# Choosing, by a table, which engine multiplies half spectra and gate products in a recurrence-then-convolution kernel

## The chip, the cores and the metric

The kernel runs on one core of a Trainium2 chip. Time is the device time of one launch in microseconds; lower is better. The kernel before takes 476.47 us, the median of 3 runs (476.25 to 478.01).

A core has five engines that run their own instruction streams in order and wait for each other by semaphores: PE (TensorE, matrix products, writes PSUM; its weight loads are listed as PEld), DVE (VectorE), ACT (ScalarE), POOL (GpSimd) and SP (SyncE), which here issues the transfers. In this kernel only DVE and ACT read PSUM; POOL works on SBUF alone.

## The reference

For each of 4 batches of 6272 time steps and 256 channels, a gated linear recurrence, then a long convolution with a filter as long as the sequence, between two projections, with a product of three factors:

```
sig = 1.0 / (1.0 + np.exp(-f_logit))
f = lower_bound[None, None, :] + (1.0 - lower_bound[None, None, :]) * sig
i = 1.0 - f
for t in range(S):
    h = f[:, t] * h + i[:, t] * x[:, t]
    y[:, t] = h
...
proj = x @ w_proj                      # x is the y above
x1, x2, x3 = (proj[..., :D].copy(), proj[..., D:2 * D].copy(), proj[..., 2 * D:].copy())
X2 = np.fft.rfft(x2, n=S, axis=1)
H = np.fft.rfft(filter_fft, n=S, axis=0)[None, :, :]
x2_conv = np.fft.irfft(X2 * H, n=S, axis=1)
y = x1 * x2_conv * x3
return (y @ w_out).astype(np.float32)
```

## The kernel before

The sequence length 6272 is 49 x 128. The Fourier transform of each channel is made of two short transforms done as matrix products, over the 128 first and over the 49 then, with a column order that needs no twiddle factors between them. Channels are taken in 16 units u of 8 pairs.

The stages of one batch, with the names that stand in the code:

- `hgrn` (lines 299 to 357), 13 chunks of up to 512 steps: SP loads f_logit and x into FL and XT (`load`); ACT makes the sigmoid (L311); POOL multiplies the two (`u`, L313); PE transposes both into PSUM (`su`, L325); ACT, or sometimes DVE, makes the factor f in fTs (L338, L340); DVE scans along time into HA (`scan`, L346). HA holds the states in f16. The first 3072 of them are copied behind the last one (`wrap`, L354 to L357), so that a strided read may pass the end; this is done by POOL or ACT.
- `phase_p` (L664): PE projects the states with the middle third of w_proj, in 13 groups (`P`, L673); ACT or DVE copies PSUM into X2 (`x2`).
- `phase_f1` (L681): PE makes the first transform of unit u (`F1`, L686); ACT or DVE copies it into A (`A`), a ring of NA = 4 units that lies inside HA. `mini` (L694) makes the zero frequency for four units together.
- `unit` (L729): the product with the filter's spectrum. SP loads the spectrum Hu of the unit from DRAM if it is not held (`H`, L723; NH = 3 buffers). PE makes the second transform (`F2`, L745) into two PSUM banks, one for each half o. DVE multiplies each bank by Hu, reading every spectrum value twice, into PP (`prod`, L758; NP = 2 buffers). POOL fills the one column left out (`slot`, L750). PE makes the first inverse transform (`I2`, L768), which needs both halves and the slot; ACT or DVE copies it into Th (`Th`).
- `gate` (L360), 13 chunks and two halves of the channels: PE makes x1 and x3 (`x13`, L373), each into one PSUM bank; ACT or DVE copies both to x1s and x3s in f32 (`xs`; x1 is scaled by ZS), two buffers in turn; POOL multiplies them into zt in f16 (`z`, L389).
- `phase_o` (L789), 13 groups: PE makes the second inverse transform (`I1`, L802); DVE multiplies PSUM by zt into ys (`y`, L808), for which all 26 z products of the batch must be done; PE multiplies by w_out (`proj`, L820); ACT or DVE scales into osb (`o`, L272), three buffers; SP stores (`store`, L830).

`prepare` makes the tables and the filter's spectrum once and puts it to DRAM, 16 units; its PE stages `rot`, `FF1`, `FF2` and `last` run beside `hgrn(0)`. It has 32 groups of four `warm` matmuls (L561) on PE, whose output nothing reads.

None of this is emitted in the order in which it is written. `Plan.op` records each step with its cost on each engine that may do it, what it reads and writes (`r`, `w`, from which its predecessors follow), how many PSUM banks it takes (`take`) and whose banks it reads (`src`). `Plan.emit` then walks through ORDER, a string that packs, for every step, its number, its engine and its PSUM bank. So ORDER sets the engine of each step and the order of each engine's instructions, and the costs have no effect when the kernel is built. In the order before, P of batch b+1 follows the output stage of batch b, the gate's steps are strewn among the units, and `hgrn(b + 1)` begins among the last units of batch b and runs on beside its output stage. The states of batch b are overwritten chunk by chunk, after the gate has read them.

In the order before, DVE does all 128 `prod`, 104 scans, 52 `y`, 19 `x2` and 23 `xs`; ACT does 185 `xs`, 86 `f`, 57 `A`, 61 `Th`, 46 `o`, 33 `x2`, 52 sigmoids and 17 wraps; POOL does 104 `z`, 52 `u`, 64 `slot` and 31 wraps. The 32 warm groups all come before the P of batch 0.

Of the kernel before, what the change touches and what calls it, by code (L numbers as in the profile page):

```python
# [13 lines left out]
AOP = mybir.AluOpType  # L14
# [7 lines left out]
S = 6272  # L22
D = 256
M = 128
Q = 49
# [14 lines left out]
HS = 64.0 / S  # L40
# [18 lines left out]
class Plan:  # L59
# [3 lines left out]
    ENGINES = ("ACT", "DVE", "PE", "POOL", "SP")  # L63

    def __init__(self):
        self.ops, self.writer, self.readers = [], {}, {}
        self.batch = 0

# [49 lines left out]
    "A8gAAYBBgAOYABIAjQBLgACIBGgAtRBQgBVgAhSBagBkgAdTA7YAPIAxUBfgA9AA2VBpgAwWBCAA0XBugBDQA+SBFABMYBzgAyUBEAARIAvV"  # L118
    "BHYBACAqWA/CBNUA1XAQAB4gAmQERgBIRBWYAkWAcTBRAADgAYYAuXAnQBJBAgWBKBESgBSWAzTBUGBbYBXQBTGEpgAeSBYIBgYASABcSBPE"
    "BlIEdgAaYBZABhWBqABOMBmQEegBeKBdCBvYBrUBjOBnAEqgAUIBoAB0YAGgBwSBiOA4QATIBxCB5YB1WByKAFgAlRBsMB2GB6SAiQB7CBtM"  # L120
    "B8CA5RETAB3OAfQAWICISCBUCJKCKQEUYB/WCLACRSCCECAOA3QEfACNUAEYCOMCDYEVWErAEZQEgYEWGCEUE1gEaAE2gEXOCFEEbIEsYEhW"
    "ElUEiGCTQFBgCSCEjOFCgANACaSCQgAVYEmECMYCUIEtWCbCEnMAIACVYCWQAXYE3AExSEuOApUFNgAHAEyKArVE4YFOgCXACcUCHgEzKCGg"
    "AJAA6QFDAClQEvOE5SALACdEFEYCmIE9WE6CCjUE+OFZgAKAFagAsQE7KCkECYgCsQAMACeYFFUFPAEcYE/OCfSFGEFQYCgCFJWFHMFjgFKG"
    "CoSFkgCtACuUFLOCPgEwYCpCFRQE0YCvMFbAFVWCnYFSIC3SFtgFcYFWOFugAoUC4CCigC1UFTICZgCxSC2EFXOC6UCyCFAYFdQCwYFlAFMY"
    "FgSC7MC+WC5YF3gE8AFmYFhKF4gDAUC/GChgFeIDBECqgDJWCzgFfIAbUFvADCYFnUDKGFiKDDQFwYFoEFqWDEAFpMDHSGBgCrgDQQDICC0g"
    "FrODSUGCgFIYDRADbSFsOF5ADLYDMQDTMFxWDcCF6YDNIDVUFyGF0SDWEFzODZQGLgF1CC8gDiUFUYC9gDaADkWF2KGMgDUYDjEDdYDtQDGg"
    "B9YGDADFgDeUDlOF7SDuADfMDnWF8CDmYF+QDoGF9KD2UGEYGVgF/ADXgDrWDOgD3ED0SDsOD/UGWgD1CGAIDwWB+YDPgFYAGNADvYGFSD4Y"
    "EAMEoYD9QDxGGGKDggD5UGOYDhgGHKD+AGIWDYgD6EEGQMVgGJOEISDzgEHAGKOEBYGPUGXAEYAGSQEJCGQMECWGTAMhgEKYGYYGRMEPSDqg"
    "EDGDpgAZYEQCGUIGZWELUGaGEkYGcSJSQGbOGdCMtgEMEGeKJTRDygGfgEEgGmWJVJJUAENgMXAD8gJWYG4SGnOGgUEFgEOgG2QG5KD7gG0W"
    "G3AGhMGsSMjAGyQGtKG1GGqUMvAGiWGrMGkSGjGHLgGoUGlKHEgMigGwWGpEMWgHSgGuSGxGJXUGvKGzAJYVJcWJaFJdXJZMG8QJfHJeOJbY"  # L130
    "G6SG9AG+UG7KJhXJgYG/EHAQJiWHBAHFSJkOJmUJjHHHKJnVJoEJlYHCQHMWJpFHIKJrUJqYJsSJtEHDIJwVHZgJuCHiTHOOHGYJxQJvYHjD"
    "J1RJyNJ2SJzAHJTHPOJ3BJ0YHgVJ4CHTQHKDHqgHNYJ6XHUYHVIHhFJ5YHkSJ7UHlCHWIHQVJ/QJ9EHbYHRNHaSHxgJ8HKARKBAJ+YHcKHmU"
    "KCBHrWHnEMkYHdKHXQKESHYAHtOH4gHeUKGCIGQHuOKDYHfEHoSKFWIHAHyUHpKH/gKJXKHGH0MMugHsYIIQKLHKIYHvSIJAH1MH5WHzYHwC"
    "H6YIKQMYYH7OIQgKKUILAH2SH8OIAVH3CIMQICNKMEIXgH9SINAKNYKOXIDNKPUH+CKTVIBYKQHIOQIegIRSIPIKVFIsWKREITKIEQItGKSY"
    "KUVIUKKYUKWFKZSISYKaEKXYIYWIlgIFAKdVIaOKbCKeTIZYIVQKfFKcYIbOKgDIfUIWAKiSIhMI2gIuWIcQIvGIiMImTInYKkCKhYI3WIpL"
    "IdAI9gKjVKnSIgYKlFIwQIoLKpCKmYIjUIxAKoSJEgI5OKsTMwYKqCIqQIkEI6OKtSIrAMZUKvKKuDI+WJLgKrYMaEMdQJAOIySMeAM5gKwY"
    "M6gIzCMbMKxWKzGMlSMfIKyUMmCK2VJBOK0EK3WK4FMpQK1YK5GMnKI0UNFgMqAMxWK6YNGgI1MM7AM1SMrIK7UMgYNRgMyGK8VI4YNSgI/Y"
    "K9EM8YMzOI7QM2CLAUK+FM3KJFWI8ALBVLCEK/YJHOM9QLDFNBSNHALEYJIOLFUNdgM+ALGVNegLHENIYM/IJCWNCCLKUNTANDKJMQJDGJGY"
    "JOINJSNUYLIFNNWNKCJPINngNOGNogNfANLKLJYNVQLMELLVNPOLPUNWANgYNZSLRELNFNXILQUNxgNaCJJWNygLSERSVNbKLOYJKGNhQNpA"
    "NkWJNYNiILTYRTUN7gNlGRUNJQSN8gNqYRVENjIRXVJRCRYUNmORZFLZQRaELUSNzAMsYLaINrUNuWNsEN0YLVKOFgLbQNvGOGgNtMLWSLcA"  # L140
    "McYNwON9ALeULjQLXCN+YLfMN1WM0AN4SLYgLkIN2GLdgLoUOPgN5CN3OOQgLgQOHANAAN6KOIYLlWLhALpMLtSLigLmGN/QLuKNQYOCUOAA"
    "LqWOagMoAOBIOZgODELngLySLrGOEMOJQORAOMWLsgLzKLvUUVgONGOSYOKAOOOL0SLwEOLIL3WM4YObAOTULxgNMAL4ONEYOWQOUENYYUhg"
    "L1COcYOVML8WUigOXAOdSL2gL9OL5UOeCNcAOfKL+WL6EOYIOgSUXAMBUOhKMGQOiKL/GOrSMHIMAgOvWOsCMCMUugOnQUWgOwGUtgO5SL7g"
    "OoAOzUO6KOlWO0EOjQOmOOxSOkAOpUUjAO1WOqMOyCMDQO2GO7SMEIOtUO8CMLWOuEMQQO3SMMOUvAMIUO4CUwYMNWMRIMJMO9QMOGO/SO+I"
    "PBUPACRWYPDWPCMPHQPEGRbYPNSPJIPFWRcURdVReEPGORhQRfFPKIPgWRjARgYRiUPhGRmVPQKPZgPiQPIYRkEPLWPjAPPKPTTPUYRlYRoF"
    "PaQPVLPqgPMGRnSRrVPOYRpCPWLPRWRtFPmSPSGPbYPcIRqYPkUPxgPnCPXWPdIRsQPlEPrSPYGRwRP4gPtKPoURuAPeWRyBPpMRvYRxQPuK"
    "PyRRzAPsYQGUPfGPzYUYYP1JP/gR1QQHEPvWP0JP5SR3AQIUPwGP7KR0YQQgP2QQJEQAWP8KP6YP3AQKUQBYR2SQLEQCOP9QQXgR4CR6TQDO"
    "QRUP+AR5YR7WR8DQTMQMQQegR9GUkYR/SMPgQNAQEWQUMQYTSBCQFGQOQSASQaLQlgR+YSEVMKgSCCSFWQPIUZSSDYSGFQbLQuQSHGSJXQvA"
    "QSYUaKQsVSIYQ2gSKUSLPQtFQVQUbKQZYSOXSMEQfVQWASNYSPUQhNSQHQwSSREQcQQxCQiNQmUQnYSSYQdAQySQpMQ9gUdWQzCQgYSTQQoM"
    "UeGSURQjSSVAUfOREgSWBQqUU5gQkCSXYU6gQ0QQ3WQ1IUgAMFgQ+SQrEQ5OQ/YSYQSZRSaASdURAKSbBSeVSfEUlQScYQ6OSgFSiWUmASjS"  # L150
    "Q4YSkGRBKShYRLgSnUSlCSoVU7AQ7WUnISmYRFSSqFSpMQ8GU8YUpQRHKSsVUqAVFgStUVGgSuFRCWRIKSvESxSSrYRDGSyVUrIRMTSwYUxW"
    "S0FRPLU1QSzCUyGS2VRGYVRgS1YROLS3SVSgS4FS7US5CS8VRNYUzOVHARJSS6YU2AS+NRQWVIYRKCU3ITAVRRGU9SS9ETBQU+KTCFVBWS/Y"
    "TDIVTAVJUVdgU/KTFRVegTEYVCGTGQTHBVDOVNSTIAVUYTKRVKEVngTLQTMBVogVLMMSWVOCTNATPRVPKTJYVVUTQQVWEMTOTOYVZSTRJTSA"
# [738 lines left out]
```

## Time and profile before

| | |
|---|---|
| median of 3 runs | 476.47 us (476.25 to 478.01) |
| span of the profiled execution | 476.4 us, mean granted clock 0.998 |
| PE, DVE, ACT, POOL busy | 447.8, 424.9, 416.1, 297.9 us |
| DMA | 112.88 MB, of it 80.93 MB read from and 31.00 MB written to HBM |
| P of batch 0, 1, 2, 3 begins in the chain of waits at | 78.8, 178.3, 282.8, 386.7 us |

The span is that of one execution under the profiler, from its first to its last instruction. An engine's busy time counts stretches in which at least one of its instructions runs; instructions that follow each other closely overlap a little in the records, so the sum of their durations is larger than the busy time, above all on PE, whose ends are modelled. In a group of instructions the columns are line, engine, operation, output and inputs, count, then busy time and mean duration of one, then the idle time of the engine just before them and what ended it. In the chain of waits each row is a start, a length and what was running.

### The profile page before, as it was taken

What the parts mean: (1) busy time and instruction counts of PE and PEld (TensorE: products, weight loads), DVE (VectorE), ACT (ScalarE), POOL (GpSimd) and SP (SyncE); (2) the same over time, 40 slices, a digit from 0 to 9 for tenths busy, and PEclk for the clock granted to TensorE, in tenths of its full rate; (3) what the DMA queues carried; (4) which work ended last, traced back from release to release, by engine and by line L of the source; (5) the groups of instructions that cost most, each with busy time, mean ns of one, the idle gap of its engine ahead of it and who ended that gap; (6) DMA issues with size and microseconds to landing.
All of it is one profiled execution on the core that took longest, in us unless ns stands there. A gap on an engine that the chain in (4) does not pass through costs nothing.

```text
span 476.4 us, 14713 instructions
## 1 busy us (share of the span) xinstructions
PE 447.8 (94%) x6041; PEld 345.4 (72%) x6041; DVE 424.9 (89%) x457; ACT 416.1 (87%) x606; POOL 297.9 (63%) x309
## 2 busy tenths in 40 slices
PE   8888999999998999999999999999999799999995
PEld 7776777866756879776666889666767697676784
DVE  8778989799999996999999996999999877999874
ACT  5899898899999998889999978999999778999763
POOL 6777784287889730668798734688787504766600
PEclk9999999999999999999999999999999999999999
DMA  8989998636588897157769995567588831356277
GB/s 329 396 310 317 313 342 251 227 104 216 165 289 306 289 328 279 41 164 226 244 230 312 345 338 219 145 205 235 163 271 270 341 135 46 110 152 193 77 279 277
DMA packets 39841, 112.88 MB, mean 237 GB/s; under 512 B 4258, under 2 KB 6178, under 8 KB 39774
## 3 DMA queue, kind: packets, MB, share of 16 engines
q1 hardware_dynamic: 39774, 111.94, 69.0%
q8 instruction: 47, 0.77, 0.6%
q14 instruction: 20, 0.16, 0.1%
HBM read 80.93 MB, written 31.00 MB: 235 GB/s over the span
## 4 chain that ended last, share of the span: by engine, by line
PE 52%; DVE 16%; DMA 12%; POOL 6%; ACT 6%; issue 6%; SPq 0%; ACTq 0%; DVEq 0%; POOLq 0%
PE PS L373 13%; PE PS L673 9%; DVE HA L346 8%; PE PS L768 8%; PE PS L745 6%; PE PS L686 5%; DVE ys L808 5%; PE PS L325 4%; DMA XT<-in_x_dram 4%; DMA X<-in_moe_filter_fft_dram 4%; PE PS L820 3%; POOL zt L389 3%; POOL XT L313 3%; DMA out_dram<-osb 2%; DVE PP L758 2%
## 5 line engine op out<-in xcount | busy, mean ns | idle before, releaser
L389 POOL TENSOR_TENSOR zt<-x1s,x3s 128x490 f16<-128x490 f32 (+1 forms) x104 | 125.5, 1214 | 67.1 <-ACT x3s L270 33.0
L313 POOL TENSOR_TENSOR XT<-XT,FL 128x1024 f32<-128x1024 f32 (+1 forms) x52 | 116.9, 2248 | 64.7 <-ACT FL L311 41.8
L758 DVE TENSOR_TENSOR PP<-PS,Hu 98x1008 f16<-98x1008 f32 x128 | 146.5, 1198 | 4.9 <-PE PS L745 2.7
L346 DVE TENSOR_TENSOR_SCAN HA<-fTs,HA,PS 128x512 f16<-128x512 f32 (+1 forms) x96 | 112.5, 1201 | 5.1 <-ACT fTs L338 4.3
L373 PE MATMUL PS<-HA,W 128*128 128x490 f16 (+1 forms) x416 | 104.5, 368 | 1.3 <-ACT Th L270 0.6
L808 DVE TENSOR_TENSOR ys<-PS,zt 128x1024 fp32r<-128x1024 f32 (+1 forms) x52 | 58.8, 1150 | 8.5 <-PE PS L802 6.5
L820 PE MATMUL PS<-Wo,ys 128*128 128x256 f32 x392 | 57.8, 293 | 3.5 <-DVE ys L808 2.5
L270 ACT CAST HA<-PS 128x1024 f16<-128x1024 f32 x57 | 57.2, 1025 | 3.7 <-PE PS L686 3.6
L338 ACT ACTIVATE fTs<-PS,nomc 128x512 f32<-128x512 f32 (+1 forms) x86 | 56.2, 672 | 4.8 <-PE PS L325 4.3
L272 ACT ACTIVATE osb<-PS 128x1024 f32<-128x1024 f32 (+1 forms) x46 | 45.0, 985 | 16.9 <-DMA out_dram<-osb 8.7
L768 PEld LDWEIGHTS <-PP 98*128 98x128 f16 x1024 | 49.7, 98 | 11.7 <-POOL PP L750 2.1
L270 ACT COPY x3s<-PS 128x490 f32<-128x490 f32 (+1 forms) x96 | 54.6, 574 | 4.0 <-PE PS L373 1.8
L820 PEld LDWEIGHTS PS<-Wo,ys 128*128 128x128 f32 x392 | 49.3, 188 | 9.0 <-DVE ys L808 4.6
L272 ACT ACTIVATE x1s<-PS 128x490 f32<-128x490 f32 (+1 forms) x89 | 52.1, 592 | 3.9 <-PE PS L373 2.2
L373 PEld LDWEIGHTS <-W 128*128 128x128 f16 x416 | 33.4, 97 | 30.4 <-issue 8.3
L311 ACT ACTIVATE FL<-FL 128x1024 f32<-128x1024 f32 (+1 forms) x52 | 52.8, 1019 | 2.1 <-DMA FL<-in_f_logit_dram 2.0
L325 PE MATMUL PS<-iden,FL 64*128 64x64 f32 x784 | 45.8, 232 | 8.6 <-DVE HA L346 2.2
L325 PEld LDWEIGHTS PS<-iden,FL 64*128 64x128 f32 x784 | 33.7, 138 | 27.0 <-DVE HA L346 9.0
L768 PE MATMUL PS<-VA,PP 98*128 98x98 f16 x512 | 51.8, 207 | 0.6 <-POOL PP L750 0.2
L270 ACT CAST Th<-PS 128x784 f16<-128x784 f32 x61 | 50.2, 830 | 1.8 <-PE PS L768 1.2
L768 PE MATMUL PS<-VB,PP 98*128 98x98 f16 x512 | 51.6, 207 | 0.0
L673 PE MATMUL PS<-W,HA 128*128 128x256 f16 x392 | 44.6, 274 | 0.2 <-DVE HA L346 0.2
(110 smaller groups left out, 685.7 us busy)
## 6 DMA issues: line engine op xcount, KB each, us to landing
FL<-in_f_logit_dram SPq DMA_DIRECT2D x48, 512.0 KB
XT<-in_x_dram SPq DMA_DIRECT2D x48, 512.0 KB
out_dram<-osb SPq DMA_DIRECT2D x48, 512.0 KB
Hu<-H SPq DMA_DIRECT2D x55, 392.0 KB
X<-in_moe_filter_fft_dram SPq DMA_DIRECT2D x9, 512.0 KB
H<-Hu SPq DMA_DIRECT2D x16, 196.0 KB
H<-Hu SPq DMA_DIRECT2D x16, 128.0 KB
Hu<-in_moe_filter_fft_dram SPq DMA_DIRECT2D x2, 512.0 KB
```

Source lines behind the costliest of these rows:

```text
L270: nc.scalar.copy(dst, src)
L272: nc.scalar.activation(dst, src, AF.Copy, scale=scale)
L313: op("u", {"POOL": 0.1 + 0.553 * nb}, lambda e, xt=xt, ft=ft: nc.gpsimd.tensor_tensor(xt, xt, ft, op=AOP.mult), r=[("ft", k)], w=[("xt", k)])
L325: nc.tensor.transpose(bank(pb)[:, at[p] + j:at[p] + hn:nb], src[ps, j, cols], iden[ps, ps])
L346: nc.vector.tensor_tensor_scan(h, fT, bank(pb)[:, 512 - hn:512 + hn], init, op0=AOP.mult, op1=AOP.add),
L373: nc.tensor.matmul(PS[:, p, 0:n], W13[:, kh, js], HA[:, HB[kh] + t0:HB[kh] + t0 + n], start=(kh == 0), stop=(kh == 1))
L389: nc.gpsimd.tensor_tensor(late["zt"][:, jb, :, m0:m0 + nm], xs(0), xs(1), op=AOP.mult),
L673: nc.tensor.matmul(pp[:, r - r0, :], column(HB[kh], q_of(r)), W2[:, kh, :], start=(kh == 0), stop=(kh == 1))
L758: nc.vector.tensor_tensor(PP[:TB, k, o, :, :, 1:64], px.unsqueeze(1).broadcast_to([TB, 2, UE, 63]), hh[:, :, :, 1:64], op=AOP.mult)
L768: nc.tensor.matmul(PS[:, ib + o, pr * TB:(pr + 1) * TB], PP[:TB, k, o, n, 2 * pr:2 * pr + 2, :], v[:TB], start=(n == 0), stop=(n == 1))
L808: nc.vector.tensor_tensor(late["ys"][:, yk, :, 0:rn * 128], PS[:, cb:cb + 2, 0:rn * 128], late["zt"][:].rearrange("p k r m -> p k (r m)") ...
L820: nc.tensor.matmul(po[:, i, :], late["ys"][:, yk, kh, i * 128:(i + 1) * 128], Wo[:, kh, :], start=(kh == 0), stop=(kh == 1))
```

## The change

Three things become possible, and a new ORDER chooses among them for each step. `Plan` gets a further engine name, MUL, which means DVE multiplying straight out of PSUM; `plan.direct()` tells, while a step is recorded, whether ORDER gives it to MUL.

1. A half spectrum can be copied (ACT or DVE) to SBUF in f16, over the unit's own place in A, and POOL then multiplies it by Hu (`pm`). Where the half goes to MUL, the product is the old one and `pm` emits nothing. New names `Ax` stand for these places, so that F1 of a later unit waits for `pm`. So that the f16 copy keeps its scale, FT is made smaller by FS = 1/8, and the filter's spectrum larger by the same.
2. x3 can be multiplied by x1s out of PSUM on DVE, into zt. Where it is, there is no x3 copy and `z` emits nothing.
3. A wrap can be a transfer, SBUF to SBUF, issued by SP.
4. ORDER is new as a whole.

```diff
-HS = 64.0 / S
+FS = 1.0 / 8.0
+HS = 64.0 / S / FS
...
-    ENGINES = ("ACT", "DVE", "PE", "POOL", "SP")
+    ENGINES = ("ACT", "DVE", "PE", "POOL", "SP", "MUL")
...
+        self.engine = {i: e for i, e, _ in self.order()}
+
+    def direct(self):
+
+        return self.engine.get(len(self.ops)) == "MUL"
...
+    def Ax(u):
+
+        return [("Ax", u % NA, o) for o in range(2)]
...
+        elif e == "SP":
+            nc.sync.dma_start(dst, src)
...
-                op("wrap", {"POOL": 0.05 + (z - t0) / 1015.0, "ACT": 0.08 + (z - t0) / 1200.0},
+                op("wrap", {"POOL": 0.05 + (z - t0) / 1015.0, "ACT": 0.08 + (z - t0) / 1200.0, "SP": 0.46},
...
+                def x3_out(e, p, xs=xs, n=n, zd=zd):
+                    px = PS[:, p, 0:n].rearrange("p (m r) -> p r m", r=Q)
+                    if e == "MUL":
+                        nc.vector.tensor_tensor(zd(), px, xs(0), op=AOP.mult)
+                    else:
+                        copy(e, xs(1), px)
+                op("xs", dict(either(n), MUL=0.07 + n / 960.0), x3_out,
+                   r=["cv"] + ([("x1s", j, 0)] if direct else []),
+                   w=[("z", jb, c) if direct else ("x1s", j, 1)], src=x13[1])
+
+                def z_out(e, xs=xs, zd=zd, direct=direct):
+                    if not direct:
+                        nc.gpsimd.tensor_tensor(zd(), xs(0), xs(1), op=AOP.mult)
...
-                pool.tensor_scalar(FT[:, 0, i, 0:98], in0=tt[i], scalar1=low, scalar2=None,
-                                   op0=AOP.mult)
+                pool.tensor_scalar(FT[:, 0, i, 0:98], in0=tt[i], scalar1=low, scalar2=FS,
+                                   op0=AOP.mult, op1=AOP.mult)
...
-           w=At(u), src=f1)
+           w=At(u) + Ax(u), src=f1)
...
+        spec = A[:TB, ka:ka + UE].rearrange("p i r k -> p (i r k)").rearrange(
+            "p (o i k) -> p o i k", o=2, k=64)
...
+            def prod(e, xb, o=o, hh=hh, pr=pr):
+                px = PS[:TB, xb + o, :]
+                if e == "MUL":
+                    px = px.rearrange("p (i k) -> p i k", k=64)[:, :, 1:64]
+                    nc.vector.tensor_tensor(
+                        pr, px.unsqueeze(1).broadcast_to([TB, 2, UE, 63]), hh, op=AOP.mult)
+                else:
+                    copy(e, spec[:, o].rearrange("p i k -> p (i k)"), px)
+            op("prod", {"MUL": 1.11, "ACT": 0.47, "DVE": 0.6}, prod, r=[("Hu", h)] if direct else (),
+               w=[("P", k, o) if direct else ("Ax", u % NA, o)], src=f2, part=o)
+
+            def late_prod(e, o=o, hh=hh, pr=pr, direct=direct):
+                if not direct:
+                    nc.gpsimd.tensor_tensor(
+                        pr, spec[:, o, :, 1:64].unsqueeze(1).broadcast_to([TB, 2, UE, 63]), hh,
+                        op=AOP.mult)
+            op("pm", {"POOL": 2.27}, late_prod,
+               r=() if direct else [("Hu", h), ("Ax", u % NA, o)], w=[("P", k, o)])
```

What the new ORDER chooses, against the old one, in numbers of instructions over the whole kernel:

| step | before | after |
|---|---|---|
| spectrum product, direct on DVE | 128 | 97 |
| half spectrum copied by ACT, by DVE | 0, 0 | 29, 2 |
| spectrum product on POOL | 0 | 31 |
| x1 and x3 copies on ACT, on DVE | 185, 23 | 137, 23 |
| x1 times x3 on POOL, on DVE | 104, 0 | 56, 48 |
| wraps on POOL, ACT, SP | 31, 17, 0 | 34, 7, 7 |
| x2 copies on ACT, DVE | 33, 19 | 25, 27 |
| output copies on ACT, DVE | 46, 6 | 51, 1 |
| filter spectrum copies on ACT, DVE | 13, 4 | 16, 1 |
| warm groups before P of batch 0, between it and P of batch 3, after that | 32, 0, 0 | 6, 20, 6 |

Of the warm groups between, 6 lie before P of batch 1, 4 before that of batch 2 and 10 before that of batch 3. The other steps that may go to two engines move by one or two. PE's other instructions, the loads and the stores are the same in number and in size.

## The prediction

> **What bounds the kernel now.** I read the page's first part for the totals, then the busy time of each engine in four stretches cut where the projection P of each batch begins in the chain of waits (78.8, 178.3, 282.8 and 386.7 us), then groups by line and shape for prices, then the chain and the waits around the one place where the four engines are fullest.
>
> ```profile
> span 476.4 us, 14713 instructions
> ...
> PE 447.8 (94%) x6041; PEld 345.4 (72%) x6041; DVE 424.9 (89%) x457; ACT 416.1 (87%) x606; POOL 297.9 (63%) x309
> ```
>
> ```profile
> 78.80:178.30 99.50, 95.30 (x1375) 72.43 (x1374) 93.53 (x95) 92.34 (x138) 67.58 (x62) 1.00 0.74 243
> 178.30:282.80 104.50, 100.69 (x1441) 77.61 (x1441) 96.60 (x96) 95.74 (x140) 67.14 (x61) 1.00 0.71 241
> 282.80:386.70 103.90, 98.92 (x1401) 75.95 (x1402) 96.33 (x95) 92.69 (x137) 68.74 (x64) 1.00 0.69 231
> 386.70:476.40 89.70, 82.67 (x1055) 64.24 (x1054) 70.62 (x72) 67.48 (x94) 35.63 (x42) 0.99 0.45 156
> ```
>
> The columns are length, then busy PE, PEld, DVE, ACT, POOL, the granted clock, the DMA share and GB/s. In the three full stretches DVE is busy 93 to 94% and ACT 89 to 93%, while POOL has a third free. PE reads 95%, but with matmul ends that overlap: six 128x490 matmuls follow each other in 1.24 us in the chain (207 ns each) where a single one is listed at 371 ns. So PE has room that its busy figure hides, and the engines that empty PSUM, DVE and ACT, set the pace. The first 78.8 us are different: the DMA share is 0.93, 0.89, 0.96 and 0.88 in 0 to 20, 20 to 40, 40 to 60 and 60 to 78 us, and the loads of the first batch and of the filter pass there.
>
> ```profile
> L758 DVE TENSOR_TENSOR PP<-PS,Hu 98x1008 f16<-98x1008 f32 x128 | 146.5, 1198 | 4.9 <-PE PS L745 2.7 <-issue 0.9 <-ACT x3s L270 0.6
> L389 POOL TENSOR_TENSOR zt<-x1s,x3s 128x490 f16<-128x490 f32 x96 | 117.4, 1230 | 66.8 <-ACT x3s L270 33.0 <-DVE ys L808 16.4 <-DVE x1s L277 10.6
> L313 POOL TENSOR_TENSOR XT<-XT,FL 128x1024 f32<-128x1024 f32 x48 | 113.9, 2374 | 59.8 <-ACT FL L311 36.9 <-DMA XT<-in_x_dram 17.9 <-PE PS L325 3.8
> L808 DVE TENSOR_TENSOR ys<-PS,zt 128x1024 fp32r<-128x1024 f32 x48 | 57.1, 1211 | 6.8 <-PE PS L802 4.9 <-PE PS L820 1.5 <-ACT x1s L272 0.2
> L270 ACT COPY x3s<-PS 128x490 f32<-128x490 f32 x89 | 51.2, 580 | 3.2 <-PE PS L373 1.8 <-POOL zt L389 0.3 <-ACT fTs L338 0.3
> L750 POOL TENSOR_TENSOR PP<-zp 98x32 f16<-98x32 f16 x64 | 20.5, 338 | 13.3 <-PE PS L768 9.4 <-DVE zp L708 3.8
> L270 ACT CAST afs<-PS 128x512 fp32r<-128x512 f32 x23 | 13.4, 593 | 2.2 <-PE PS L615 1.4 <-POOL mX L624 0.4
> L275 DVE COPY x3s<-PS 128x490 f32<-128x490 f32 x7 | 4.6, 654 | 0.7 <-POOL zt L389 0.6
> ```
>
> These are the prices. The first row is the spectrum product that the change can divide, the second the product that it can take from POOL.
>
> ```profile
> 229.00:254.00 25.00, 24.23 (x341) 15.68 (x339) 24.13 (x27) 23.50 (x41) 23.20 (x21) 1.00 0.76 257
> ```
>
> ```profile
> 250.81 1.93 POOL zt L389 x2
> ...
> 252.94 1.03 POOL zt L389
> ...
> 253.99 1.24 DVE ys L808
> ```
>
> Here, at the end of the gate of batch 1, all four engines are 93% busy or more, and the first y product on DVE (253.99) starts when the last z on POOL ends. So POOL, idle on average, is on the path just before each output stage.
>
> **The change part by part.** The numbers of instructions are counted in the new order string.
>
> Spectrum products. 31 of 128 half spectra leave the direct DVE product (31 x 1.198 = 37.1 us off DVE). 29 are copied by ACT (nearest row: ACT from PSUM, 512 columns, 593 ns: +17.2 us), 2 by DVE (0.67 us for that shape: +1.4), and all 31 are multiplied by POOL. POOL's two shapes of L313 (1024 columns 2374 ns, 256 columns 734 ns) give 187 ns plus 2.135 ns a column; that predicts 1233 ns for the 490 columns of z, which measure 1230, so the type of the output is not the matter. For 1008 columns it gives 2.34 us. The only POOL product with two f16 inputs is L750: 338 ns for 32 columns, against 255 by the line, 2.6 ns a column more; taken whole that makes 1008 columns 4.96 us. Below, the cheapest POOL row is a one-input copy of 512 f16 columns at 612 ns, 1.2 us for 1008. I take 2.34, nearest by length and by inputs: 31 x 2.34 = +72.5 us on POOL.
>
> x3 products. 48 of 104 z products move into DVE: 48 x 1.23 = 59.0 us off POOL, 48 x3 copies off ACT (48 x 0.58 = 27.8), and 48 products of 490 columns out of PSUM on DVE. L808's shapes (1211 ns for 1024, 419 for 256) give 155 ns plus 1.031 ns a column, 660 ns; the strided x3 copy on DVE is 654. So +31.7 us on DVE, with bounds 0.58 (the ACT copy) and 0.75 (the 512-column DVE scale from PSUM, 740 ns, rounded up), 28 to 36 us.
>
> Wraps. 10 fewer on ACT (10 x 0.622 = 6.2 off), 3 more on POOL (+1.8), 7 as DMAs. Each of the 7 waits on SP for a scan, with loads, spectrum loads and stores of the neighbouring batches queued behind it. SP already waits 137 us in all for spectrum buffers freed by DVE products, in order, so a wait for a scan that is due earlier adds nothing unless a load behind it is the next one missing. A landing of 128 KB is between 2 and the 4.1 us that one spectrum load takes in the chain; wraps concern chunks 0 to 5 of 13, so seven more chunks of scans (2 x 7 x 1.2 = 17 us of DVE) lie before the P that reads them. Cost nothing; without that cover 2 to 4 us for each of two batches.
>
> Reassignments. By the counts: x2 copies +8 on DVE (1.236) and -8 on ACT (1.044), output copies -5 on DVE (1.22) and +5 on ACT (1.027), filter spectra -3 and +3 (1.217 and 1.024), and single swaps of f, A, Th, filter copies. Together +0.3 us on DVE and +0.2 on ACT; two filter copies leave POOL (-2.1).
>
> Warm matmuls. 26 of 32 groups leave the first 78 us: 6 in stretch one, 4 in two, 10 in three, 6 in the last, of which 5 stand behind the last projection. A group of four takes 0.47 us (20 matmuls in 2.36). The 20 in the full stretches are 9.4 us of PE; their cover is PE's idle time there, 4.2 + 3.8 + 5.0 = 13.0 us. Cost nothing; without the cover up to 9.4.
>
> The new dependency. A ring slot now stays held until POOL has read the copied spectrum, and the inverse I2, in order on PE, waits for POOL. In the 29 units with a copied half, the PE order puts on average 5.3 us of matmuls (priced at the spacing of the rows) between the forward matmuls F2 and I2, and under 3.5 us in one. Copy and product take 0.59 + 2.34 = 2.93 us, 4.2 with one z ahead on POOL. So covered; two z or an L313 product ahead are not.
>
> Sums: DVE -37.1 + 1.4 + 31.7 + 0.3 = -3.7 us. ACT -27.8 + 17.2 - 6.2 + 0.2 = -16.6. POOL -59.0 + 72.5 + 1.8 - 2.1 = +13.2. PE and DMA bytes the same.
>
> How much of it reaches the end: the front stays at 78.8, since 22.8 MB instead of 23.4 stand ahead of the last load of batch 0, and the last output stage keeps its 13 steps. In between, if only DVE counts, its -3.7 over its busy share of 0.93 gives -4.0. If evacuation could be shared freely, (3.7 + 16.6)/2 over 0.93 gives -10.9. The order string keeps DVE's load almost where it was, so the first is nearer; of ACT's relief I take a third of the 4.7 us for which DVE scans wait for ACT's f, -1.5. So -5.5 us: a span of 470.9. The median of the runs is 476.47 against a span of 476.4, so 0.1 lies around it: 471.0.
>
> **The rivals.** *Evacuation evens out fully*: ACT's slack is used everywhere, 476.5 - 10.9 = 465.6. For it: PE's room and the POOL chain at 254 that loses 48 products. Against it: DVE stays at 92% or more, and its stretches of scans and y products contain nothing that was taken away.
>
> *No gain: PE takes DVE's place.* PE's cover of 13.0 us takes the 9.4 us of warm groups badly, since a bank must be free for each; if 5 us of them stand in PE's way, the gain is used up: 476. For it, PE idles in short pieces, the longest wait 1.6 us. Against it, those pieces lie mostly where DVE alternates scans and y products.
>
> *Slower: I2 waits for POOL.* Products on POOL of 3.7 us instead of 2.34 make 0.59 + 3.7 + 1.23 for one z ahead = 5.5 us; with a second instruction ahead half of the time some 0.6 more, against a cover of 5.3, so each of 29 units stops PE by about 0.4 to 0.8 us, and with it the DVE and ACT work behind. At 0.6 that is +17.4 - 5.5 = +12: 488; at the lower end 483. It decides from about 3.4 us a product. For it: L750's price and POOL's fullness before each output stage (23.2 of 25 us). Against it: z's f16 output costs nothing extra, and neither does an f16 copy (612 ns for 512, where f32 copies of 256 and 1024 at 452 and 1053 give 652).
>
> *Slower: a cold front.* The first 30 warm matmuls take 6.17 us, 206 ns each, later ones 118, though the granted-clock column says 1.00 for both. With 6 groups instead of 32, the front's other PE work, 69.4 us busy less 15 for warm groups = 54, could run at 206/118 of its time, 95 us, and end some 16 us late: 487. Against it, filter transforms are dense from 24 us on and PE is needed for them anyway.
> The Trainium skill, "TensorE: Matmul & The Clock Gate", Part 1, says that the array runs at half clock until about 3.4 us of sustained work and falls back after an idle window; the slow first 6 us agree, and by that rule alone the loss here would be a few us, since dense transforms release the clock themselves.
>
> That the change doesn't do what it says is out: the decoded order holds 31 POOL products and 48 DVE ones.
>
> **How the numbers follow.** Forecast 0.52, full evening-out 0.09, no gain 0.14, late POOL 0.20, cold front 0.05. The forecast's own range is 466.5 to 475. About 0.5%, 2.4 us, is what a measurement of this kernel can tell from no change: faster below 474.1, slower above 478.9. Faster: 0.46 of the forecast's 0.52 and 0.09, 0.55. Same: the 0.06 left of the forecast, 0.09 of no gain, 0.02 of a mild late POOL, 0.17. Slower: 0.05 of no gain, 0.18 and 0.05, 0.28. The range of 464 to 486 leaves out the mildest tenth below and half of the bad cases above.
>
> **What would show it.** Right: POOL's product of 98x1008 at 2.2 to 2.5 us, the 128x490 DVE product from PSUM at 0.65, DVE busy 419 to 423 us, ACT 400 to 404, POOL 308 to 314, P of batch 0 beginning within 2 us of 78.8, and L768's waits for POOL products under 3 us in all. Wrong: I2 waiting for POOL in most units, P of batch 0 later than 82 us, warm matmuls in the chain, or DVE and ACT both with more idle time than now in the stretches between.

## The result and the profile after

The changed kernel takes 483.0 us (median of 6 runs, 479.16 to 485.08) against 476.73 us for the kernel before (476.25 to 478.01). The ratio is 1.0121 with a 95% interval of 1.0084 to 1.0157: slower by 6.3 us, where 5.5 us faster was forecast. The time lies inside the wide range of 464 to 486, outside the forecast's own 466.5 to 475, and on the wrong side of the old time.

The totals of the page after:

```profile
span 481.9 us, 14698 instructions
...
PE 448.9 (93%) x6041; PEld 351.8 (73%) x6041; DVE 419.3 (87%) x476; ACT 406.6 (84%) x581; POOL 304.4 (63%) x293
```

VectorE lost 5.6 us of work, ScalarE 9.5, GpSimd gained 6.5, and the span grew by 5.5 us. Where it grew is read from the starts of the projection P, and from the four stretches between them (columns as before: length, busy PE, PEld, DVE, ACT, POOL, granted clock, DMA share, GB/s):

```profile
87.10:186.40 99.30, 95.52 (x1394) 74.79 (x1393) 92.92 (x97) 88.32 (x132) 68.14 (x57) 1.00 0.74 244
186.40:290.20 103.80, 100.41 (x1461) 79.49 (x1457) 97.01 (x101) 90.63 (x131) 72.02 (x60) 1.00 0.70 245
290.20:394.50 104.30, 101.31 (x1467) 80.68 (x1464) 95.19 (x101) 90.78 (x130) 72.41 (x59) 1.00 0.70 236
394.50:481.90 87.40, 83.82 (x1056) 65.09 (x1055) 69.45 (x77) 64.73 (x88) 33.37 (x36) 1.00 0.45 161
```

From the start of P of batch 0 to the end they make 394.8 us, where the profiled execution of the kernel before needs 397.7 (476.4 - 78.7): 2.9 us less. But P of batch 0 begins at 87.1 us instead of 78.7. So the front lost 8.4 us, and everything behind it won back a third of that. In the front, the three windows of 10 us that differ most, first in the kernel before, then in the changed one:

```profile
10.00:20.00 10.00, 8.89 (x70) 7.40 (x68) 7.88 (x16) 9.89 (x16) 8.83 (x11) 1.00 1.04 398
20.00:30.00 10.00, 9.43 (x93) 7.45 (x93) 6.90 (x12) 8.57 (x13) 5.59 (x8) 1.00 0.89 351
30.00:40.00 10.00, 8.38 (x131) 7.05 (x129) 9.37 (x10) 9.35 (x16) 8.10 (x8) 1.00 0.89 277
```

```profile
10.00:20.00 10.00, 3.26 (x14) 2.66 (x14) 6.61 (x24) 8.96 (x12) 4.49 (x8) 0.50 1.03 413
20.00:30.00 10.00, 6.35 (x31) 5.03 (x30) 5.37 (x9) 6.21 (x12) 8.34 (x10) 0.82 0.61 238
30.00:40.00 10.00, 8.29 (x69) 7.19 (x70) 3.42 (x5) 9.27 (x12) 5.13 (x7) 0.52 0.46 153
```

TensorE does 14 matmuls instead of 70 in the first window, and its granted clock is 0.50. The DMA share falls from 0.89 to 0.61 and 0.46. ScalarE is busy for 24.4 us of the three windows instead of 27.8, VectorE for 15.4 instead of 24.2: from 10 to 42 us it waits 11.3 us for TensorE's results and 3.3 us for ScalarE's factors. What ScalarE does there stands in its timeline, first before, then after (start, length, line, operation; lines of other copies left out):

```profile
10.79 1.28 ACT L521 ACT_TABLE_LOAD   x1
...
12.63 1.03 ACT L270 CAST afs<-X 128x1024 fp32r<-128x1024 f32 x1
...
15.81 0.65 ACT L521 ACTIVATE PP<-PP 128x512 f32<-128x512 f32 x1
...
23.49 1.28 ACT L311 ACT_TABLE_LOAD   x1
```

```profile
13.37 1.28 ACT L551 ACT_TABLE_LOAD   x1
14.66 0.64 ACT L551 ACTIVATE PP<-PP 128x520 f32<-128x520 f32 x1
15.21 0.58 ACT L281 CAST f<-PS 128x512 fp32r<-128x512 f32 x1
15.81 1.28 ACT L324 ACT_TABLE_LOAD   x1
17.11 1.06 ACT L324 ACTIVATE FL<-FL 128x1024 f32<-128x1024 f32 x1
18.07 1.03 ACT L281 CAST afs<-X 128x1024 fp32r<-128x1024 f32 x1
...
30.88 1.28 ACT L551 ACT_TABLE_LOAD   x1
32.17 0.63 ACT L551 ACTIVATE PP<-PP 128x512 f32<-128x512 f32 x1
32.82 1.28 ACT L324 ACT_TABLE_LOAD   x1
34.11 1.06 ACT L324 ACTIVATE FL<-FL 128x1024 f32<-128x1024 f32 x1
```

L551 (before L521) is the sine of the tables, L324 (before L311) the sigmoid of the states. The new order takes them in turns: sine, sigmoid, sine, sigmoid, and each change of function is a table load of 1.28 us. The kernel before does both sines first and has two such loads in the same place, at 10.79 and 23.49 us. The cast that comes at 18.07 us, behind the first sigmoid and its load, came at 12.63. On TensorE after, the matmuls that wait for that cast, the first filter transform (L645), and the first transposes of the states (L338); below, the last two in the kernel before:

```profile
19.15 2.08 PE L620 MATMUL PS<-afs,rot 128*128 128x256 f32 x8 [5.59 <-ACT afs L281]
...
30.91 2.08 PE L645 MATMUL PS<-D1r,f 128*128 128x256 f32 x8 [2.59 <-ACT f L281]
32.92 0.69 PE L338 MATMUL PS<-iden,FL 64*128 64x64 f32 x8
```

```profile
24.26 2.59 PE L615 MATMUL PS<-D1r,f 128*128 128x256 f32 x20
...
27.78 0.41 PE L325 MATMUL PS<-iden,FL 64*128 64x64 f32 x8
```

TensorE idles 5.59 us waiting for that cast, and the first filter transform starts at 30.91 us instead of 24.26; its eight matmuls take 2.08 us, where twenty took 2.59 before. SP issues no load between 20.07 and 34.62 us, where the kernel before pauses from 21.66 to 29.16: the buffers for f_logit and x are full until the first chunk is transposed, and in TensorE's order that stands behind the first filter transforms (32.92 us instead of 27.78). That the first sigmoid runs earlier than before, at 17.11 us, doesn't help.

The two new instructions cost, by their groups in the page after:

```profile
L805 POOL TENSOR_TENSOR PP<-HA,Hu 98x1008 f16<-98x1008 f16 x31 | 65.1, 2104 | 10.1 <-ACT HA L281 8.0 <-DMA Hu<-H 1.1 <-PE PS L815 0.9
L408 DVE TENSOR_TENSOR zt<-PS,x1s 128x490 f16<-128x490 f32 x42 | 27.3, 658 | 1.6 <-ACT x1s L283 0.8
```

### The profile page after: what moved, and what is told of

Its sections match the earlier page's. It is cut to its first block, busy times and chain, and to the rows that moved or that the text cites. A ratio compares the mean times of both kernels' runs of the same rounds, so it can differ in the third digit from the quotient of the medians.

```text
span 481.9 us, 14698 instructions
## 1 busy us (share of the span) xinstructions
PE 448.9 (93%) x6041; PEld 351.8 (73%) x6041; DVE 419.3 (87%) x476; ACT 406.6 (84%) x581; POOL 304.4 (63%) x293
## 4 chain that ended last, share of the span: by engine, by line
PE 62%; DMA 11%; DVE 10%; ACT 9%; issue 3%; POOL 3%; SPq 0%; DVEq 0%; ACTq 0%; POOLq 0%
PE PS L387 16%; PE PS L815 9%; PE PS L703 7%; PE PS L775 6%; PE PS L338 6%; DVE HA L359 6%; PE PS L716 6%; PE PS L867 5%; DVE ys L855 3%; PE PS L849 3%; DMA FL<-in_f_logit_dram 3%; DMA H<-Hu 3%; DMA Hu<-H 2%; ACT X L281 2%; DMA XT<-in_x_dram 2%
## 5 line engine op out<-in xcount | busy, mean ns | idle before, releaser
L796 DVE TENSOR_TENSOR PP<-PS,Hu 98x1008 f16<-98x1008 f32 x97 | 113.5, 1199 | 6.3 <-DMA Hu<-H 2.7
L387 PE MATMUL PS<-HA,W 128*128 128x490 f16 (+1 forms) x416 | 101.5, 367 | 2.5 <-DVE PP L796 1.3
L417 POOL TENSOR_TENSOR zt<-x1s,x3s 128x490 f16<-128x490 f32 (+1 forms) x56 | 68.1, 1224 | 35.9 <-ACT x3s L281 11.9
L281 ACT CAST HA<-PS 128x1024 f16<-128x1024 f32 (+1 forms) x85 | 72.7, 876 | 6.2 <-PE PS L716 3.6
L805 POOL TENSOR_TENSOR PP<-HA,Hu 98x1008 f16<-98x1008 f16 x31 | 65.1, 2104 | 10.1 <-ACT HA L281 8.0
L283 ACT ACTIVATE osb<-PS 128x1024 f32<-128x1024 f32 (+1 forms) x51 | 49.2, 977 | 17.3 <-PE PS L867 9.9
L351 ACT ACTIVATE fTs<-PS,nomc 128x512 f32<-128x512 f32 (+1 forms) x88 | 57.6, 674 | 5.4 <-PE PS L338 4.0
L387 PEld LDWEIGHTS <-W 128*128 128x128 f16 x416 | 35.5, 97 | 33.0 <-issue 8.1
L324 ACT ACTIVATE FL<-FL 128x1024 f32<-128x1024 f32 (+1 forms) x52 | 52.7, 1017 | 3.5 <-DMA FL<-in_f_logit_dram 3.3
L815 PEld LDWEIGHTS <-PP 98*128 98x128 f16 x1024 | 49.1, 98 | 9.0 <-issue 2.3
L283 ACT ACTIVATE x1s<-PS 128x490 f32<-128x490 f32 (+1 forms) x85 | 49.3, 594 | 5.7 <-PE PS L387 4.8
L815 PE MATMUL PS<-VA,PP 98*128 98x98 f16 x512 | 52.1, 207 | 0.3 <-DVE PP L796 0.2
L815 PE MATMUL PS<-VB,PP 98*128 98x98 f16 x512 | 51.7, 207 | 0.0
L338 PE MATMUL PS<-iden,FL 64*128 64x64 f32 x784 | 45.2, 233 | 1.5 <-DVE HA L359 0.4
L338 PEld LDWEIGHTS PS<-iden,FL 64*128 64x128 f32 x784 | 34.3, 141 | 14.7 <-DVE HA L359 2.9
```

What stands on the lines that cost most here:

```text
L281: nc.scalar.copy(dst, src)
L283: nc.scalar.activation(dst, src, AF.Copy, scale=scale)
L338: nc.tensor.transpose(bank(pb)[:, at[p] + j:at[p] + hn:nb], src[ps, j, cols], iden[ps, ps])
L387: nc.tensor.matmul(PS[:, p, 0:n], W13[:, kh, js], HA[:, HB[kh] + t0:HB[kh] + t0 + n], start=(kh == 0), stop=(kh == 1))
L417: nc.gpsimd.tensor_tensor(zd(), xs(0), xs(1), op=AOP.mult)
L796: nc.vector.tensor_tensor(pr, px.unsqueeze(1).broadcast_to([TB, 2, UE, 63]), hh, op=AOP.mult)
```

## The experiments

The kernels differ from the one before or the changed one in ORDER, which also names the engine of each step, and in the number of warm groups, and in nothing else; line numbers move by a few with it. Since ORDER is packed, the edits are shown as decoded steps. "P0" is the first matmul of P of batch 0, "behind" the rest of the span, both from the profiled execution. The ratio is to the kernel before, run on the same chip. One execution is not all: the same order up to P0 gives a P0 of 78.7 to 81.2 us in s0, s1, s2, s3 and s5, and the same order behind P0 gives 395.9 to 399.3 us in the kernel before, e4, e6 and e7. So the run times, with their intervals, weigh more than a difference of 1 or 2 us between two profiles.

| label | edit | P0 | behind | median us (lowest to highest) | ratio (95%) |
|---|---|---|---|---|---|
| (before) | | 78.7 | 397.7 | 476.73 (476.25 to 478.01) | 1 |
| (after) | | 87.1 | 394.8 | 483.0 (479.16 to 485.08) | 1.0121 (1.0084 to 1.0157) |
| e1_warm | after, warm groups back in front | 87.6 | 398.5 | 486.12 (482.24 to 489.33) | 1.0200 (1.0154 to 1.0246) |
| e2_tables | after, sines together | 81.7 | 395.5 | 479.54 (476.64 to 485.13) | 1.0058 (1.0031 to 1.0086) |
| e12_both | both | 90.2 | 398.2 | 487.39 (486.44 to 490.38) | 1.0237 (1.0212 to 1.0263) |
| e4_before_cold | before, 6 warm groups | 80.4 | 399.3 | 479.28 (475.7 to 483.84) | 1.0036 (1.0011 to 1.0062) |
| e6_before_tables | before, functions in turns | 80.7 | 396.7 | 481.79 (479.36 to 484.98) | 1.0078 (1.0051 to 1.0105) |
| e7_before_both | before, both of these | 82.4 | 395.9 | 481.65 (480.32 to 484.11) | 1.0110 (1.0082 to 1.0137) |
| s0_splice | front of before, rest of after | 81.2 | 395.3 | 477.94 (473.96 to 480.34) | 1.0003 (0.9977 to 1.0028) |
| s1_no_mid_warm | s0, no warm groups in the rest | 81.0 | 393.7 | 477.87 (475.89 to 483.01) | 1.0021 (0.9989 to 1.0052) |
| s4_warm_p0 | s0, two more warm groups ahead of P0 | 79.0 | 395.4 | 476.38 (474.41 to 480.21) | 0.9980 (0.9956 to 1.0005) |
| s5_wraps_act | s0, the 7 wraps by DMA on ScalarE | 78.7 | 397.8 | 478.83 (476.44 to 483.8) | 1.0031 (1.0002 to 1.0061) |
| s2_no_pool | s0, 27 of 31 POOL products on VectorE | 78.8 | 429.5 | 509.39 (507.36 to 511.55) | 1.0658 (1.0621 to 1.0694) |
| s3_no_dve_z | s0, x3 products copied and on POOL again | 79.8 | 463.0 | 544.08 (541.97 to 546.14) | 1.1381 (1.1345 to 1.1417) |

**Is it the cold TensorE or the turns of functions? Repairs in the changed kernel.** The two theories were that the 26 warm groups taken out of the front leave TensorE at half rate, and that ScalarE's new order delays the casts. e1 puts the groups back ahead of the same front steps as in the kernel before:

```diff
-PE: 6 warm, 13 rotations, FF1 FF1 su su FF1 ...  (20 warm later, 6 at the end)
+PE: 6 warm, rot, 2 warm, rot, 2 warm, rot, 3 warm, rot, 5 warm, rot, ...  (32 in front)
```

> The changed kernel with 26 of its 32 warm groups put back among the filter transforms of the front, where the kernel before has them, so none is left between the batches. Cold theory (the array runs at half rate through the front's first transforms because too little runs on it): the first eight FF1 matmuls take 1.6 us instead of 2.07, and P of batch 0 begins 3 to 8 us earlier than at 87.1, total 475 to 480. Table theory (ACT loads its tables four times beside the first load and the transforms wait for it): P of batch 0 moves by under 2 us, total 481 to 484. If the warm groups between the batches stood in PE's way, the stretches after P of batch 0 get shorter by up to 9 us in all; if they lay in idle time, by under 2.

It was a miss: P0 stayed at 87.6 us, though the clock rose to 0.83 in the window from 10 to 20 us and 1.00 in the next. The groups were no cover here, they got in the way: sixteen of their matmuls run in one go from 15.4 to 18 us after 2.2 us of waiting for a bank that VectorE empties. Most of the 3.1 us by which the run is slower than the changed kernel is lost elsewhere: P0 is 0.5 us later, and the part behind it, which has lost its warm groups, takes 398.5 us instead of 394.8, with the clock at 0.98 in its second and third stretch. The three runs with a mean clock of 0.983 to 0.985 take 487.9 to 489.3 us, the three with 0.991 to 0.995 take 482.2 to 484.3, like the changed kernel. So e1 does not say what the cold clock of the front costs. e2 leaves the groups alone and changes ScalarE's order:

```diff
-ACT: ... first sine, cast, sigmoid 0, 15 casts, second sine, sigmoid 1, ...
+ACT: ... first sine, 3 casts, second sine, 12 casts, sigmoid 0, cast, sigmoid 1, ...
```

> The changed kernel with the second sine of the filter tables put right behind the first on ACT and the first sigmoid moved behind the filter's copies, as in the kernel before, so that two table loads (2.6 us) go; the warm groups stay where the change put them. Table theory: FF1 begins 4 to 6 us earlier than at 30.9, P of batch 0 at 80 to 83, total 476 to 479. Cold theory: FF1 begins a little earlier but its matmuls stay slow, P of batch 0 at 85 or later, total 481 to 483.

```profile
14.98 1.22 PE L620 MATMUL PS<-afs,rot 128*128 128x256 f32 x4 [2.94 <-ACT afs L281]
...
29.20 2.07 PE L645 MATMUL PS<-D1r,f 128*128 128x256 f32 x8 [3.14 <-ACT f L281]
```

The wait for the cast falls from 5.59 to 2.94 us, and P0 moves from 87.1 to 81.7: in the profiles the turns of functions and the casts queued behind them are 5.4 of the 8.4 us, with the clock still at 0.53 and 0.50 in the windows from 10 to 30 us. By the run times it is less, 3.5 us (483.0 to 479.54), or 0.63 of the 1.21%. e12 does both edits.

> Both edits together. If front and nothing else is the loss, P of batch 0 begins at 78 to 81 and the total is the 476.5 of the kernel before less the 2.8 us that the later stretches gained, 472 to 476. If the two causes cover each other, each alone gives little and both give it all. If the front is slow for a third reason (the order of the loads), P of batch 0 stays at 83 or later.

The warm groups hurt again, and here in the front: P0 is at 90.2 instead of 81.7, and the first filter transform starts at 31.86 us instead of 29.20.

**The same two parts, put into the kernel before.** This is the complement, in an order in which the warm groups fit. e4 leaves out 26 of 32 groups ("WARM = 32" becomes "WARM = 6").

> The kernel before with only its first 6 warm groups, the other 26 left out; nothing reads their output. Cold theory: the granted clock falls in the first 40 us, the rotations and first FF1 slow down, P of batch 0 begins 2 to 8 us later than at 78.8, total 478 to 484. Table theory: P of batch 0 within 1 us of 78.8, total 475 to 477.5.

P0 moves by 1.7 us to 80.4, with the clock at 0.70 from 10 to 20 us and 0.50 from 20 to 30, and the time by 0.36%, also 1.7 us. e6 changes ScalarE's order, and with it the one product on POOL that reads the second sine. The sigmoid moves ahead of four casts (the expectation's six is a miscount):

```diff
-ACT: ... second sine, 10 casts, sigmoid 0, 2 casts, sigmoid 1, ...
+ACT: ... 6 casts, sigmoid 0, 4 casts, second sine, 2 casts, sigmoid 1, ...
```

> The kernel before, its front edited only in ScalarE's order: the first sigmoid of the states moves ahead of six filter copies and the second sine behind the last filter copy, so that ScalarE goes sine, sigmoid, sine, sigmoid as in the changed kernel; the sine's dependent copy of the table moves behind the first gate product on POOL. WARM stays 32. Theory (the alternation of functions delays the front by itself): two more table loads, 2 x 1.28 us, on ScalarE ahead of the first filter transforms; P of batch 0 begins 2 to 5 us later than 78.7, at 81 to 84, and the time is 478.5 to 481.5 (ratio 1.004 to 1.010). Rival (it was costly in the changed kernel only because its TensorE was cold and its casts already late): P of batch 0 within 1.5 us of 78.7, time 476 to 478.

P0 moves by 2.1 us, about the 2 x 1.28 us of the two added loads. The time moves by 0.78%, 3.7 us; the profiled execution (479.36 us) is the fastest of the eleven. So the turns cost in a front with all its warm groups too, where the clock is 1.00 up to 30 us and 0.83 in the window behind. e7 has both edits at once and asks whether they feed each other.

> The kernel before with both suspected parts of the new front at once: ScalarE goes sine, sigmoid, sine, sigmoid, and 26 of the 32 warm groups are left out (WARM 6). Alone they moved P of batch 0 by +2.2 us and +1.7 us. Theory (each costs its own share, the rest of the changed kernel's 8.4 us lies in its other front order): P of batch 0 at 78.7 + 2.2 + 1.7 = 82.6 us, within 1; time some 480.5 to 483. Rival (the two feed each other: late casts keep TensorE idle and at half rate, and that keeps the buffers of the loads full, and this makes up the changed kernel's front): P of batch 0 at 85 to 87.5, time 484 to 487.

P0 is at 82.4: 3.7 us late, where the two alone add up to 3.8. The times agree: 1.10% (0.82 to 1.37), where the two alone make 0.36 and 0.78. They add and do not multiply; the rival of a loop between them falls. By the times the two come near the whole loss of the front, 1.18% between the changed kernel and the splice s0 below.

In the order of the kernel before they make 3.7 of the 8.4 us in the profiles. In the changed kernel the first sigmoid's load comes earlier among the casts, at 15.81 us (20.11 in e6), and the turns cost 5.4 us there; of the other 3.0, 1.7 us for the cold clock would leave 1.3. Of these, 0.8 us need be no loss: the new order has eight matmuls of the gate ahead of P0 instead of four (1.81 us in s4, 1.00 before). The rest is a difference between two kernels' fronts and was not measured by itself; the changed order of the loads, whose first is one of f_logit ahead of the filter's, lies in it, and no run changed that alone.

**Is the rest of the change worth what was forecast?** The splice s0 takes the front of the kernel before (its order up to P of batch 0, with 32 warm groups) and then the changed order for all else, its 26 later groups included ("WARM = 58").

> The front (filter transforms, loads, first recurrence, 32 warm groups) in the order of the kernel before, everything behind it in the new order, with its 26 warm groups between the batches and at the end kept (58 groups in all). If the loss lies in the front alone: P of batch 0 begins at 78.5 to 80.5, the stretches behind it take the 394.8 us that the changed kernel's take, total 473 to 476, 0.2 to 0.8% faster than the kernel before. If the later stretches only looked shorter because a late front had filled their buffers: they take 397 or more, total 476 to 479.

The time is that of the kernel before, 1.0003 where the changed kernel has 1.0121: the changed front makes the loss, about 1.2%. Behind P0 the profile is 2.4 us shorter (395.3 against 397.7), and P0 is 2.5 us later. Of that delay 0.8 us are the four further gate matmuls, and 1.4 us a stretch of half clock, seen on TensorE:

```profile
76.97 0.23 PE L339 MATMUL PS<-iden,XT 64*128 64x64 f32 x2
78.17 3.24 PE L388 MATMUL PS<-HA,W 128*128 128x490 f16 x8 [0.98 <-DVE HA L360]
81.20 2.98 PE L704 MATMUL PS<-W,HA 128*128 128x256 f16 x23
```

Eight matmuls of the gate take 3.24 us, at a granted clock of 0.55 to 0.60 from 78 to 82 us. s4 puts two warm groups (eight matmuls) into the 0.98 us of waiting ahead of them:

```diff
-PE: ... su, x13, x13, x13, x13, P ...
+PE: ... su, warm, warm, x13, x13, x13, x13, P ...
```

> The splice (front of before with its 32 warm groups, rest of after) with two more warm groups on TensorE in the idle 0.98 us ahead of the first gate projections of batch 0 at 78 us (WARM 60). Theory (the half-clock window at 78 to 82 us follows from TensorE's idle time at 74 to 78 and delays P of batch 0 from 78.8 to 81.2): the two groups fill the gap, the clock stays at 1.00, P of batch 0 begins at 79 to 80, and the median is 475 to 476.5 (ratio 0.997 to 1.000 with the splice at 1.0003). Rival (the window has another cause, or it is hidden behind VectorE's work anyway): the clock dips again or the median stays at 477.5 to 478.5.

```profile
76.27 1.05 PE L592 MATMUL PS<-iden 128*128 128x256 f16 x8
77.32 1.81 PE L388 MATMUL PS<-HA,W 128*128 128x490 f16 x8
78.97 5.29 PE L704 MATMUL PS<-W,HA 128*128 128x256 f16 x47
```

The eight gate matmuls now take 1.81 us and P0 is at 79.0. The median of 476.38 lies in the 475 to 476.5 expected, but the intervals of s4 and s0 overlap, and s2, s3 and s5 below, with the gap of 0.98 us left in, also show 1.81 us in their profiled executions. So the dip moves P0 by 1.4 us when it comes (3.24 against 1.81; s3, whose gate matmuls start within 0.03 us of those of s0, has P0 at 79.8 instead of 81.2); that the two groups prevent it is not shown. s4 is the best version run; it does not beat the kernel before beyond the measurement.

s1 takes the 26 later warm groups out of s0 and nothing else ("WARM = 32").

> The same as the splice, without the 26 warm groups behind the front (32 left, all in the front). If those groups keep the array's clock up where PE would otherwise pause, the granted clock falls below 1 somewhere between 200 and 420 us and the total is 2 to 5 us above the splice's. If they only fill idle time, it is the same within 1 us; if they stand in PE's way, it is up to 9 us lower.

477.87 against 477.94 us: the groups behind the front neither help nor cost anything that can be measured here (the runs of s1 have a mean clock of 0.994, those of s0 0.996; that the groups hold the clock up a little is neither shown nor ruled out). s5 returns one part of the change, the wraps by DMA:

```diff
-wrap (7 of 52): SP
+wrap (7 of 52): ACT
```

> The splice with its seven wraps by DMA put on ScalarE instead, at the same places of the order. ScalarE gets 7 x 0.62 = 4.4 us more work in batches 1 to 3. Theory (behind the first projection only VectorE's busy time sets the pace, so that ScalarE's relief brought nothing): no change, ratio within 0.003 of the splice's 1.0003. Rival (ScalarE's relief and the wraps by DMA carry part of the 2.9 us gained behind the first projection): 1 to 4 us slower than the splice, ratio 1.003 to 1.009.

The theory's own bound, within 0.003 of the splice, is just met (1.0031 against 1.0003), and the intervals overlap. But in the profiles the part behind P0 takes 397.8 us instead of 395.3, and compared at the same mean clock of 1.000, five runs of s5 average 477.6 us, five of s4 475.8 and three of s0 475.7. At a mean clock of 0.996 s5 is 1.1 us behind s0 and 2.2 behind s4. So the 4.4 us of wraps on ScalarE cost some 1 to 2 us, and the better reading, though not a proof, is the rival's: ScalarE's relief carries part of the gain. At the wraps its queue also waits for VectorE's scan, 1.5 us once:

```profile
L282 ACT COPY HA<-HA 128x512 f16<-128x512 f16 x17 | 10.6, 625 | 1.5 <-DVE HA L360 1.5
```

s2 and s3 return the other two parts, in the changed order. s2 gives 27 of the 31 products on POOL to VectorE again, direct from PSUM, as early as their inputs allow.

> The splice with 27 of its 31 POOL spectrum products given back to DVE out of PSUM at the place of the copy or, where that can't be, as soon as what it needs is there (4 stay on POOL, where the bank is needed at once). DVE gains 27 x 1.2 = 32 us of work, ACT loses 15 and POOL 57. If DVE sets the pace in the stretches between, 8 to 30 us slower than the splice. If I2's waits for POOL cost as much as DVE's relief brings, within 2 us; if they cost more, faster.

The time grows by 31 us, for 27 products of 1.20 us, 32 us, more on VectorE (its busy time grows by 28.4): nearly one for one. s3 gives the 48 x3 products back to a copy on ScalarE and a product on POOL.

> The splice with all 48 DVE products of x1 and x3 given back: x3 copied by ACT, the product on POOL right behind it. DVE loses 32 us of work, ACT gains 28 and POOL 59. If the pace is DVE's alone, faster by up to 10 us; if DVE and ACT empty PSUM as one pool of work, with POOL's z at the end of the gate on the path, 5 to 25 us slower.

66 us more, where POOL gets 48 x 1.23 = 59 us, and ScalarE 28. TensorE's clock falls to 0.93 and 0.92 in the second and third stretch, so part of this may be half clock, and how much isn't known. Both say that the new order is built around these engines and has no room to take the work back. Neither says what the parts are worth against an order made without them: the kernel before does without them in 476.7 us.

## Why the forecast was wrong, step by step

**The front stays at 78.8: failed, and this is the step that turned the sign.** P0 came at 87.1 us, and the prediction had named "later than 82" as a sign of being wrong. It was argued from the bytes ahead of the last load. Bytes did not set it, since the buffers were full: loads stop for 14.5 us because the transposes of the first chunk are late behind the filter transforms. The prediction counted how many copies change their engine in the front, and left out in which order ScalarE runs functions of two tables. Two more loads of 1.28 us are a small number, but the first of them, with a sigmoid, stands ahead of a cast for which TensorE waits 5.59 us, and e2 gets 5.4 us of P0 and 3.5 us of time back by order alone. With the front of the kernel before (s0) the loss is gone.
The Trainium skill has the rule that spoke against this, "ScalarE: Activation LUTs", in its section "Table sets: the hidden batching unit": do all calls of one set together, then those of the next. The runs e2 and e6 agree with the rule. Under "What ACT_TABLE_LOAD costs" it prices a change of set at some 2.66 us, of which 1.38 us are a drain; here the load takes 1.28 us and the next activation follows 0.01 us after it (14.66 after 13.37 + 1.28), so no drain shows.

**Warm groups cost nothing: half right.** Between the batches no cost can be measured (s1 against s0). What was taken from the front was not free: 1.7 us of P0 in e4, ratio 1.0036.

**Cold front, the rival at 0.05: right in kind, too large in size.** It priced all 54 us of front work at half rate, 16 us. In the changed kernel the clock is 0.50, 0.82 and 0.52 in the windows from 10 to 40 us, but 0.97 in the next, where 120 matmuls run instead of 69; in e4 it is 0.70, 0.50 and 0.94, and 1.7 us of delay came of it. The rival that was missing is the order of functions on ScalarE.

**Prices of the new instructions: right for VectorE, near for POOL.** The VectorE product was put at 0.66 and measures 658 ns. The POOL product was put at 2.34, with bounds of 1.2 and 4.96, and measures 2.10 us: L750's price was mostly a fixed cost: the changed kernel's two rows of f16 products on POOL, 339 ns for 32 columns and 2104 for 1008, make 1.81 ns a column, as an estimate, and 281 ns ahead of them.

**I2 waits for POOL: the rival fell.** It needed 3.4 us a product. In the waits after, those of I2 (L815) that end on POOL are 0.3 us for the slot's product and 0.2 put down to a gate product; none is for L805.

**The sums: one near, two mis-sized.** POOL was forecast at +13.2 and shows +6.5; the product's price, 31 x 0.236 = 7.3 us less, covers the difference of 6.7. VectorE was forecast at -3.7 and shows -5.6, of it -2.5 behind P0. ScalarE was forecast at -16.6 and shows -9.5: -13.8 behind P0, and 4.3 more ahead of it, where the added loads are 2.6.

**The middle gains 5.5 us: right in sign, less than half in size.** The splice and the changed kernel show 2.4 and 2.9 us behind P0 against one profile of the kernel before, and that one is long: with the 1.9 us between span and time (below) its 476.4 us stand for a run of some 478.3, as an estimate, above all six runs beside the changed kernel. Over the executions with the same order behind P0, the old one takes 397.7, 399.3, 396.7 and 395.9 us (before, e4, e6, e7) and the new one 394.8, 395.5, 395.3 and 395.4 (after, e2, s0, s4). The means differ by some 2 us, and by the run times the best splice, s4, is 0.2% faster, inside its interval. That VectorE's 2.5 us come back one for one, as the first of the two terms said, is not shown: the three full stretches are together 0.5 us shorter with 1.3 us less on VectorE, the last is 2.3 us shorter with 1.2 less. Nor is it known what ScalarE's 13.8 us of relief brought; that wraps as DMAs cost nothing holds, and s5 puts them at some 1 to 2 us of gain. The third stretch is 0.4 us longer than before with 1.1 us less on VectorE, and TensorE's idle time in the three full stretches is 10.2 us instead of 13.0.

**PE takes VectorE's place: not borne out as written.** Its 5 us were to come from the warm groups among the batches, and s1, without them, is no faster than s0. They do show in the chain, as the prediction's sign of being wrong had it, but late: 0.45 us at 475.92 us, and 2.20 us behind the last projection. The longest wait of TensorE in the kernel before was 1.4 us; the prediction's 1.6 is one of VectorE for TensorE.

**From span to time: a step off, without effect on the result.** The runs with both figures show 1.9 us between them (483.82 against a span of 481.9), not 0.1; the profiled execution of the kernel before was not its median one.

## What to carry to other kernels

When a change brings a new order of all steps, read the start-up as carefully as the steady part: list what each engine runs there in order, and count ScalarE's changes of function and what is queued behind each. Bytes in flight said nothing here about a front whose buffers were full. And parts can be split by splicing one kernel's front to another's rest, which here put the whole loss on the front in one run. A profile is one execution: P0 and the part behind it vary by 2 to 3 us from one to the next, as much as most of the effects here.

## What was not expected of the hardware

A half-clock stretch need not follow a long pause. In s0 it came at 78 us after waits of 0.67, 0.46 and 0.98 us within 4 us. Of five executions with the same TensorE order and like waits up to there, two show it (s0, s1) and three do not (s2, s3, s5). In s0 the clock is 0.70, 0.50, 0.50 and 0.59 in the four windows of 1 us from 78 us, together 3.4 us at half clock; of a span of 476 us that lowers the mean clock by 0.0036. Steps of this size are seen between runs, and runs at a mean of 0.996 are 1.1 to 2.4 us longer than runs at 1.000 (s0: 478.1 against 475.7; s4: 477.0 against 475.8; s5: 479.2 against 477.6). The Trainium skill, "TensorE: Matmul & The Clock Gate", Part 1, describes a free-running window of about 3.4 us, with a moment of change that depends on where in the window the matmuls start. The length of the stretch in s0 agrees with it.

The granted-clock column of the kernel before reads 1.00 in the first 10 us, where 16 warm matmuls take 3.18 us and 20 later ones 2.36; in that stretch only the matmuls' own durations show the rate.

On POOL, the product of two f16 inputs takes 2104 ns for 1008 columns, less than the 2339 ns that the f32 products' line gives for the same length.
